# Unused space at both edges of SBUF moves where a three-stage kernel's tiles begin

## The chip, the cores and the metric

One core of one Trainium2 chip. The metric is the device time of one execution in microseconds, as a median of the runs.

## What is computed

Three stages follow one another on 2,304 tokens, all in fp32 (batch 4, 8 heads, 576 positions, head width 64; model width 512; hidden width 2,048):

```python
# attention by a feature map
proj = x @ w_phi;  proj -= max(abs(proj))
phi(x) = concat(exp(proj), exp(-proj))
kv = phi(k).T @ v;  z = sum(phi(k))
attn = (phi(q) @ kv) / (phi(q) @ z + 1e-6)
# first layer
h = x @ w_in1;  x = (h * cos(h)) @ w_out1
# second layer
h = x @ w_in2;  out = (max(h, 0) + alpha * min(h, 0)) @ w_out2
```

q, k, v, the four weights (float64) and alpha come from HBM; the host only lays out q, k and v.

## The kernel before, in words

Every fp32 product of the two layers is made of three matmuls (`mm3`, L163): each operand is split into a high and a low part (xh and xl, wih and wil, woh and wol, gh and gl), and high·high, high·low and low·high are added in PSUM. The parts have type fp32r.

The tokens stand in five groups, four of 512 and one of 256 (`groups`). The hidden width stands in 16 tiles of 128 (ft). One step is one ft for one group in one layer, 160 steps in all (`steps`). A step computes

- `hidden`: a tile ph of 128 hidden units × the group's tokens, 4 kk × 3 = 12 matmuls; the moving rows are xh or xl of one kk (512 or 256 columns), the stationary operand is a 128 × 128 slice of wih or wil;
- `turns`, `gate` and `activate` (ScalarE, VectorE), which end with gh (a ScalarE copy, L85) and gl (a GpSimd subtraction, L86);
- `output`: the products with the second weight into the PSUM tiles po. In layer 0 the moving rows are gh or gl, the stationary slices are from woh or wol, 4 × 3 = 12 matmuls; in layer 1 the moving rows are woh or wol (always 512 columns), the stationary slices are from gh or gl, 12 matmuls for a group of 512 tokens and 6 for the one of 256.

The order is written by hand (`tc.manual_schedule()`, `moe_step`): hidden runs five steps ahead of output, and on TensorE a sequence of ph matmuls follows a sequence of po matmuls. Weights are decoded from float64 by ten instructions on three engines (`w_instructions`), at times that a small planner in the kernel sets, into six slots per kind. The weight loads go through SyncE's queue (`fetch_w`).

Where a tile lies is set by the order of the pools. Pools are stacked from both ends of SBUF. From the left: `const` (small constants, w2 and ident of the attention), `small`, `xpool` (xh and xl, four rows of 2,304 fp32 each), `wst` and `wtmp` (staging of the weights), `wpool` (weight slots 0 and 1), `accp` (five accumulators), then the attention's `wk` and `qpp`, which make room later for `wpool2` (slots 2 to 5) and `wtmp2`. From the right: the attention's `vp` and `kw`, which make room later for `gp` (five gh and five gl) and `mt` (two r). A weight tile, gh, gl and r have 2,048 bytes in each partition; xh and xl have 36,864, which is 18 × 2,048.

Of the kernel before, what the change touches and what calls it, by code (L numbers as in the profile page):

```python
# [10 lines left out]
F32 = mybir.dt.float32  # L11
# [10 lines left out]
P = 128  # L22
# [6 lines left out]
def feature_map_attention_two_mlps(  # L29
# [30 lines left out]

    ctx.enter_context(tc.manual_schedule())

    const = ctx.enter_context(tc.tile_pool(name="const", bufs=1))
    small = ctx.enter_context(tc.tile_pool(name="small", bufs=2))
    xpool = ctx.enter_context(tc.tile_pool(name="xpool", bufs=1))
    wst = ctx.enter_context(tc.tile_pool(name="wst", bufs=2))
# [731 lines left out]
```

## Time and profile before

| | us |
|---|---|
| time, median of 3 runs | 998.44 (998.33 to 998.99) |
| span of the profiled execution, first to last instruction | 996.2 |
| TensorE busy | 989.7 |
| its weight loads busy | 838.6 |
| VectorE, GpSimd, ScalarE busy | 686.3, 606.4, 493.9 |

The profiled execution has its span alone, not a device time of its own; the median stands 2.2 us above the span. In the views, PE is TensorE's matmuls and PEld its weight loads, DVE is VectorE, ACT ScalarE, POOL GpSimd. L163 is line 163 of the kernel. A name like po<-gh,wol reads: the output tile, the moving tile, the stationary tile. A matmul's duration is the time from its issue to its modelled end; the next begins before that.

### The profile page before, as it was taken

How to read it: one execution, taken by the hardware profiler on the slowest of the kernel's cores; microseconds unless marked ns; L12 is line 12 of the kernel's file. 1: busy time of each engine (PE TensorE's matmuls, PEld its weight loads, DVE VectorE, ACT ScalarE, POOL GpSimd, SP SyncE). 2: the span in 40 equal slices, each digit the busy share in tenths (PEclk: the TensorE clock that was granted, in tenths of full speed). 3: DMA queues.
4: the chain of work that ended last, by engine and by line, in shares of the span. 5: the costliest groups of instructions: out<-in, count | busy, mean ns of one | idle time of the engine just before them, and what ended most of it. 6: DMA issues, size and time to landing. Idle time of an engine off the chain costs nothing.

```text
span 996.2 us, 13997 instructions
## 1 busy us (share of the span) xinstructions
PE 989.7 (99%) x5145; PEld 838.6 (84%) x5145; DVE 686.3 (69%) x976; ACT 493.9 (50%) x967; POOL 606.4 (61%) x498
## 2 busy tenths in 40 slices
PE   9999999999999999999999999999999999999998
PEld 7999999888888888888888888888888888888886
DVE  6868686668886577647764789587748774875343
ACT  5888888866666476646665663132213221322100
POOL 3577787856667366536655889477537753775221
PEclk9999999999999999999999999999999999999999
DMA  6454543211111021101110111011101110110112
GB/s 166 108 149 120 151 126 91 71 44 60 64 43 64 22 63 44 43 22 62 44 43 22 43 59 48 22 62 45 43 22 58 50 43 22 50 55 1 43 58 91
DMA packets 64580, 60.63 MB, mean 61 GB/s; under 512 B 28928, under 2 KB 54656, under 8 KB 64512
## 3 DMA queue, kind: packets, MB, share of 16 engines
q1 hardware_dynamic: 64512, 59.75, 20.0%
q8 instruction: 40, 0.66, 0.3%
q14 instruction: 28, 0.23, 0.1%
HBM read 52.50 MB, written 4.79 MB: 58 GB/s over the span
## 4 chain that ended last, share of the span: by engine, by line
PE 96%; DVE 1%; ACT 1%; issue 1%; POOL 1%; POOLq 0%; ACTq 0%
PE ph L163 39%; PE po L163 39%; PE pj L453 6%; PE kv L494 5%; PE nm L578 5%; PE tp L534 2%; PE tp L430 0%; DVE acc L243 0%; ACT acc L553 0%; DVE wt L125 0%; DVE wt L122 0%; DVE we L126 0%; ACT qp1h L567 0%; POOL wol L133 0%; POOL gl L86 0%
## 5 line engine op out<-in xcount | busy, mean ns | idle before, releaser
L86 POOL TENSOR_TENSOR gl<-r,gh 128x512 fp32r<-128x512 f32 (+1 forms) x160 | 204.1, 1277 | 305.4 <-ACT gh L85 300.4
L85 ACT CAST gh<-r 128x512 fp32r<-128x512 f32 (+1 forms) x160 | 92.1, 576 | 392.9 <-DVE r L209 266.9
L163 PE MATMUL ph<-xh,wil 128*128 128x512 f32 (+1 forms) x640 | 236.7, 370 | 0.0
L163 PE MATMUL ph<-xh,wih 128*128 128x512 f32 (+1 forms) x640 | 236.5, 370 | 0.0
L163 PE MATMUL ph<-xl,wih 128*128 128x512 f32 (+1 forms) x640 | 236.0, 369 | 0.0
L243 DVE TENSOR_TENSOR acc<-po,acc 128x512 f32<-128x512 f32 (+1 forms) x134 | 86.9, 658 | 104.7 <-PE po L163 104.1
L163 PEld LDWEIGHTS ph<-xl,wih 128*128 128x128 f32 x640 | 120.5, 188 | 22.3 <-POOL xl L622 0.2
L163 PEld LDWEIGHTS ph<-xh,wih 128*128 128x128 f32 x640 | 120.5, 188 | 22.0
L163 PEld LDWEIGHTS ph<-xh,wil 128*128 128x128 f32 x640 | 120.4, 188 | 21.3
L163 PE MATMUL po<-gh,wol 128*128 128x512 f32 (+1 forms) x320 | 119.5, 373 | 0.1
L163 PE MATMUL po<-gh,woh 128*128 128x512 f32 (+1 forms) x320 | 119.0, 372 | 0.0
L163 PE MATMUL po<-gl,woh 128*128 128x512 f32 (+1 forms) x320 | 119.0, 372 | 0.0
L163 PE MATMUL po<-woh,gh 128*128 128x512 f32 x288 | 114.0, 396 | 0.0
L163 PE MATMUL po<-woh,gl 128*128 128x512 f32 x288 | 113.6, 394 | 0.1
L163 PE MATMUL po<-wol,gh 128*128 128x512 f32 x288 | 113.6, 395 | 0.0
L122 DVE SCALAR_TENSOR_TENSOR wt<-ws,we 128x512 int32<-128x512 int32 x64 | 97.9, 1530 | 2.4
L196 DVE TENSOR_SCALAR r<-ph,al 128x512 f32<-128x512 f32 (+1 forms) x80 | 55.3, 691 | 58.0 <-PE ph L163 38.1
L131 POOL TENSOR_TENSOR wu<-wu,we 128x512 f32<-128x512 f32 x64 | 83.0, 1297 | 1.3 <-ACT wu L128 1.3
L207 DVE TENSOR_TENSOR r<-ph,r 128x512 f32<-128x512 f32 (+1 forms) x80 | 50.5, 631 | 47.8 <-ACT r L194 47.7
L569 POOL TENSOR_TENSOR qp1l<-acc,qp1h 128x512 fp32r<-128x512 f32 (+1 forms) x64 | 59.1, 949 | 26.4 <-ACT qp1h L567 26.4
L494 PEld LDWEIGHTS kv<-vm,kp 128*128 128x128 f32 x512 | 72.3, 191 | 2.6 <-ACT qp1h L567 0.4
L494 PE MATMUL kv<-vm,kp 128*128 128x66 f32 x512 | 72.2, 255 | 0.1
(81 smaller groups left out, 1876.0 us busy)
## 6 DMA issues: line engine op xcount, KB each, us to landing
ws<-in_moe_w_in_dram SPq DMA_DIRECT2D x32, 512.0 KB, 3.6
ws<-in_moe_w_out_dram SPq DMA_DIRECT2D x32, 512.0 KB, 3.5
acc<-dr SPq DMA_DIRECT2D x32, 144.0 KB, 3.0
out_dram<-acc SPq DMA_DIRECT2D x18, 256.0 KB, 2.0
vm<-in_v_dram SPq DMA_DIRECT2D x16, 256.0 KB, 3.5
kin<-in_k_dram SPq DMA_DIRECT2D x28, 128.0 KB, 2.8
qin<-in_q_dram SPq DMA_DIRECT2D x28, 128.0 KB, 2.8
acc<-acc SPq DMA_DIRECT2D x16, 144.0 KB, 2.4
```

The source lines that it names most:

```text
L85: nc.scalar.copy(hi, src)
L86: lo_engine.tensor_tensor(out=lo, in0=src, in1=hi.bitcast(F32), op=ALU.subtract)
L122: lambda: stt(out=t, in0=w1, scalar=-0x40000000, in1=e, op0=ALU.bitwise_and, op1=ALU.bitwise_or),
L131: lambda: tt(out=u, in0=u, in1=ef, op=ALU.mult),
L163: nc.tensor.matmul(ps, lhsT=l, rhs=r, start=(first and m == 0), stop=(last and m == n - 1))
L196: nc.vector.tensor_scalar(out=r, in0=ph, scalar1=0.0, scalar2=al[:, ft:ft + 1], op0=ALU.min, op1=ALU.mult)
L207: nc.vector.tensor_tensor(out=r, in0=ph, in1=r, op=ALU.mult)
L243: nc.vector.tensor_tensor(out=a, in0=po, in1=a, op=ALU.add)
L453: nc.tensor.matmul(pj[:, a].rearrange("p j f -> p (j f)"), lhsT=x[:, a * P:(a + 1) * P], rhs=w2.rearrange("p j f -> p (j f)"), start=True, ...
L494: nc.tensor.matmul(ps[:, :, y, :] if pr is None else ps[:, pr, y, :], lhsT=e[:, s, 2 * a + y, :], rhs=vt[:, y] if pr is None else vm[:, pr ...
L569: nc.gpsimd.tensor_tensor(out=dl, in0=et, in1=dh.bitcast(F32), op=ALU.subtract)
L578: nc.tensor.matmul(nm, lhsT=l[:, s, pr, y * VW:(y + 1) * VW], rhs=r[:, s, y, :], start=(s == 0 and m == 0), stop=(s == 1 and m == 2),)
```

## The change

Two tiles are allocated that no instruction reads or writes: one of 504 fp32 per partition in a new pool at the right edge, ahead of all others there, and one of 40 fp32 at the head of the left-most pool.

```diff
     ctx.enter_context(tc.manual_schedule())
 
+    edge = ctx.enter_context(tc.tile_pool(name="edge", bufs=1, side="right"))
+    edge.tile([P, 504], F32, name="edge")
     const = ctx.enter_context(tc.tile_pool(name="const", bufs=1))
+    const.tile([P, 40], F32, name="fill")
     small = ctx.enter_context(tc.tile_pool(name="small", bufs=2))
     xpool = ctx.enter_context(tc.tile_pool(name="xpool", bufs=1))
```

Afterwards x, the layers' weights and the gated tiles all begin at multiples of 2,048 bytes.

## Rows read from the trace of the kernel before

**Rows 1.** The page: the span, and busy time by engine.

```profile
span 996.2 us, 13997 instructions
PE 989.7 (99%) x5145; PEld 838.6 (84%) x5145; DVE 686.3 (69%) x976; ACT 493.9 (50%) x967; POOL 606.4 (61%) x498
```

**Rows 2.** The page: the chain that ended last, by engine and by line.

```profile
PE 96%; DVE 1%; ACT 1%; issue 1%; POOL 1%; POOLq 0%; ACTq 0%
PE ph L163 39%; PE po L163 39%; PE pj L453 6%; PE kv L494 5%; PE nm L578 5%; PE tp L534 2%; PE tp L430 0%; DVE acc L243 0%; ACT acc L553 0%; DVE wt L125 0%; DVE wt L122 0%; DVE we L126 0%; ACT qp1h L567 0%; POOL wol L133 0%; POOL gl L86 0%
```

**Rows 3.** TensorE's longest wait (us, times, longest); the page's costliest GpSimd group.

```profile
PE tp L430 <- DVE half_pi L432: 1.5, 1, 1.5
...
L86 POOL TENSOR_TENSOR gl<-r,gh 128x512 fp32r<-128x512 f32 (+1 forms) x160 | 204.1, 1277 | 305.4 <-ACT gh L85 300.4
```

**Rows 4.** Stages: us, busy us by engine, granted clock, DMA share, GB/s.

```profile
0.00:196.00 196.00, 193.75 (x1421) 178.74 (x1422) 142.49 (x241) 158.96 (x366) 138.13 (x136) 1.00 0.48 123
...
242.00:600.00 358.00, 357.95 (x1721) 298.92 (x1720) 252.95 (x350) 215.56 (x387) 227.13 (x179) 1.00 0.14 46
...
700.00:980.00 280.00, 280.00 (x1281) 231.03 (x1281) 175.02 (x231) 59.54 (x108) 143.74 (x111) 1.00 0.12 42
```

**Rows 5.** Matmuls of L163 by shape: count | busy us, mean ns | idle before.

```profile
L163 PE MATMUL ph<-xh,wih 128*128 128x512 f32 x512 | 200.5, 392 | 0.0
...
L163 PE MATMUL po<-woh,gh 128*128 128x512 f32 x288 | 114.0, 396 | 0.0
...
L163 PE MATMUL po<-gh,wol 128*128 128x512 f32 x256 | 101.3, 396 | 0.1
...
L163 PE MATMUL ph<-xl,wih 128*128 128x256 f32 x128 | 36.2, 283 | 0.0
...
L163 PE MATMUL po<-gh,wol 128*128 128x256 f32 x64 | 18.2, 284 | 0.0
```

**Rows 6.** The chain in order of time, layer 0: start us, us, what.

```profile
441.81 2.79 PE po L163 x12
444.60 2.73 PE ph L163 x12
447.33 1.44 PE po L163 x12
448.77 2.76 PE ph L163 x12
```

**Rows 7.** The same in layer 1.

```profile
702.74 2.80 PE po L163 x12
705.54 2.76 PE ph L163 x12
...
722.20 1.43 PE ph L163 x12
```

**Rows 8.** Matmuls in order of time, layer 1: start us, duration us.

```profile
702.58 0.40 PE L163 MATMUL po<-woh,gh 128*128 128x512 f32 x1
702.82 0.40 PE L163 MATMUL po<-wol,gh 128*128 128x512 f32 x1
703.05 0.39 PE L163 MATMUL po<-woh,gl 128*128 128x512 f32 x1
...
707.22 0.39 PE L163 MATMUL ph<-xh,wil 128*128 128x512 f32 x1
707.44 0.39 PE L163 MATMUL ph<-xh,wih 128*128 128x512 f32 x1
707.67 0.39 PE L163 MATMUL ph<-xl,wih 128*128 128x512 f32 x1
```

**Rows 9.** The chain in order of time, in the attention: start us, us, what.

```profile
15.39 1.30 PE pj L453 x6
```

**Rows 10.** Weight loads by shape: count | busy us, mean ns | idle before.

```profile
L163 PEld LDWEIGHTS ph<-xh,wih 128*128 128x128 f32 x640 | 120.5, 188 | 22.0
```

## The prediction

> **What bounds the kernel now.** I first read the page's busy times [rows 1]: TensorE is busy for 99% of the span, its weight loads for 84%, GpSimd for 61%. That share is modelled, so I check it against the chain that ended last [rows 2]: 96% of it is TensorE, 39% hidden products (ph), 39% output products (po), and nothing else above 6%. The third view is what TensorE waited for: 1.5 us in the longest entry, while GpSimd alone waited 300.4 us for the gated tile that it subtracts [rows 3]. The other engines have slack; TensorE has none. The fourth is the table of stages [rows 4]: the granted clock is 1.00 in every stage, the 2.4 GHz level, so no time is to be had from the clock. The attention ends at about 196 us; the two layers fill the remaining 800 us of a span of 996.2.
>
> So the time is a count of matmuls times the distance between their starts. The by-shape table gives the counts [rows 5]: 3 × 512 for ph with 512 columns, 3 × 288 and 3 × 256 for po, together 3,168; with 256 columns 3 × 128 and 3 × 64, together 576. The distance must not be read off the duration column: 392 ns is the latency of one matmul, and matmuls overlap. The chain in order of time shows it. In layer 0 twelve po take 2.79 us and twelve ph 2.73, where they follow 512-column po [rows 6], or 232.5 and 227.5 ns each; in layer 1 it is 2.80 and 2.76 [rows 7]. 512 columns at 2.4 GHz are 213.3 ns. Each matmul thus pays 14 to 20 ns over its columns, and po pays more than ph. Single starts say how [rows 8]: 240, then 230 ns at the head of a po sequence, 220 and 230 at the end of the next ph sequence (starts rounded to 10 ns). The distances wander inside a sequence although nothing is waited for.
>
> **What the change does, part by part.** No instruction, DMA, wait or buffer is added or removed; two tiles that nobody reads or writes take space. `fill` (40 × 4 = 160 bytes) lifts everything on the left that is allocated after it; `edge` (504 × 4 = 2016 bytes) lowers everything on the right. If x, the weights and the gated tiles begin at multiples of 2048 afterwards, then before x and the weights began 2048 − 160 = 1888 bytes past one, gh and gl 2016 bytes past one (all are made of whole 2048-byte pieces). From the shapes: a row of x for one kk is 2304 × 4 = 9216 bytes, so odd kk begin 1024 further; a weight slice begins at a multiple of 512 from its tile.
>
> TensorE reads two streams, the moving rows and the next weights, and only their addresses change. In ph both are on the left: their starts differ by a multiple of 512 bytes, before and after. In po one is on the left and one on the right: they differ by a multiple of 512 plus or minus 128 before (2016 − 1888), by a plain multiple of 512 after. This is the one relation that changes, and it splits the matmuls as the trace does: ph is the quicker one in both layers, although in layer 1 po has the weights as its moving rows and in layer 0 the gated tiles [rows 6, 7].
>
> Costs, step by step. The two tiles themselves: nothing, no instruction touches them. VectorE, ScalarE and GpSimd read other addresses too; whatever this is worth, up or down, lies under TensorE while the 300.4 us of slack stand [rows 3]; without that cover the 1277 ns of the GpSimd subtraction [rows 3] would come due per step, but a step of 24 matmuls lasts over 5.5 us. DMAs land at other offsets, all issued a tile ahead: nothing. Attention: no relation that I can price; I leave it at 196 us and let the range carry it.
>
> The matmuls: bounds from rows. No gain at all is one end. The other is the pace of the attention's projections, whose passes take 1.30 / 6 = 216.7 ns [rows 9], 3.4 over 213.3; they are of another number format, so this is a far row. With 216.7 for 512 columns and 110 for 256, twelve become 2.60 and 1.32. Layer 0: 64 sequences (4 groups × 16) of each kind, 64 × (0.13 + 0.19) = 20.5 us; layer 1: 64 × 0.16 + 72 × 0.20 = 24.6 (its 864 po are 72 dozens); 256 columns: 48 dozens from about 1.43 [rows 6, 7] to 1.32, 5.3. Sum 50.4. Losses are not excluded: the nearest row is the 240 ns at the head of a po sequence [rows 8].
>
> By the Trainium skill ("TensorE: Matmul & The Clock Gate", Back-to-back issue gap) a warm matmul follows the last after N / 2.4 + 2.5 ns, 215.8 for 512 columns; no 512-column matmul of these layers runs so here, and by that page the most to be had would be an estimated 53 us.
>
> I take the value nearest to the changed relation: all twelves go to the quickest that this kernel has at 512 columns, 2.73 us [rows 6]. Layer 0 po: 64 × 0.06 = 3.8; layer 1 ph: 64 × 0.03 = 1.9 (slow only in its first half, which follows a po); layer 1 po: 72 × 0.07 = 5.0. Sum **10.8 us**. The median of the runs is 998.44, the profiled span 996.2, so 2.2 us lie around the span and stay. 998.4 − 10.8 = 987.6, say **988**. What is late next is again TensorE: 10.8 us over 128 steps is 0.08 us a step.
>
> **Rivals.**
> *No effect.* The 14 to 20 ns belong to the matmul itself (its number format, its weight swap) and the wandering to the PE's own pipeline. For it: with 256 columns a ph's moving rows cross a multiple of 2048 in the even kk alone and a po's always, yet a dozen takes 1.43 and 1.44 us [rows 6, 7]. Against it: po and ph differ at 512 columns with equal shapes. Time 998.4. The Trainium skill speaks for it ("TensorE: Matmul & The Clock Gate", Step-by-step: what each phase is for): moving rows and weights have read ports of their own, and loading the next weights takes nothing from the running matmul. By that rule my 10.8 us would be zero; the trace neither agrees nor disagrees, since every matmul here has a weight load beside it [rows 10].
>
> *Full pace.* The start offset costs each matmul a fixed piece, whatever its length: 1.43 / 12 − 106.7 = 12.5 ns at 256 columns and 227.5 − 213.3 = 14.2 at 512 are nearly the same [rows 6, 7]. Before the change all these operands begin 32 bytes off a multiple of 64 (1888 and 2016 are); aligned, the piece goes in part or whole: 998.4 − 50.4 = 948 at most, half of it 973. Against it: a fixed piece is also what a swap would cost.
>
> *Lockstep (slower).* Moving rows and next weights now always begin at the same place of their 2048 bytes, or whole slices apart, and collide at their starts in every po. Price: the 240 ns of the worst po [rows 8] for all, 2.88 a dozen: 64 × 0.09 + 72 × 0.08 = 11.5 us, 1010. It decides from 0.65 ns a matmul on (2 us / 3,168). For it: the page's chain gives no reason for 240. Against it: ph has had this relation all along and is the quicker.
>
> *Inert.* An untouched tile might get no space; then 998.4.
>
> **How the numbers follow.** Settled pace (988, with half or all of the gain and a little more: 984 to 996) 0.36; no effect 0.27; full pace 0.17; lockstep 0.18; inert 0.02. About 0.2%, 2 us, is what a measurement of this kernel can tell from no change. Faster 0.36 + 0.17 = 0.53; same 0.27 + 0.02 = 0.29; slower 0.18. The range takes the first two cases whole, the full pace down to 958 (0.12 of it) and lockstep up to half its price, 1004 (0.07): 0.82 or so. The likeliest case's own range is 984 to 996.
>
> **What would show it.** Right: dozens of po at 2.73 to 2.76 in both layers, ph 2.73 in layer 1 as in layer 0, 256-column dozens still 1.43, the attention still 196 us, the granted clock 1.00. No effect: 2.79 and 2.80 stand. Full pace: 256-column dozens under 1.38 and ph under 2.70. Lockstep: po dozens above 2.82 while ph stays. I am wrong altogether if the time changes while the dozens don't: then it lies in the attention, or in a wait that TensorE has not had.

## The result, and the profile after

The changed kernel takes 988.35 us as a median of 4 runs (987.32 to 989.85), the kernel before 998.38 beside it: a ratio of 0.9896, 95% interval 0.9884 to 0.9907, that is 10.0 us less. 988 was forecast.

The page of the profiled execution, in the parts that answer to [rows 1] and [rows 2]: span and busy time, then the chain by engine.

```profile
span 987.3 us, 13997 instructions
PE 979.3 (99%) x5145; PEld 838.7 (85%) x5145; DVE 689.2 (70%) x976; ACT 494.2 (50%) x967; POOL 607.4 (62%) x498
...
PE 95%; ACT 2%; DVE 1%; issue 1%; POOL 1%; DMA 0%; POOLq 0%; ACTq 0%
```

Every count is the old one, the weight loads cost the same, and TensorE is the bound as before; its busy time alone went from 989.7 to 979.3. The duration column by shape says little of this (it answers to [rows 5]; count, busy us, mean ns): 392 ns has become 390 and 396 has become 390. It shows latency, which no sum of the time can use.

```profile
L166 PE MATMUL ph<-xh,wih 128*128 128x512 f32 x512 | 199.5, 390 | 0.0
...
L166 PE MATMUL po<-woh,gh 128*128 128x512 f32 x288 | 112.4, 390 | 0.0
...
L166 PE MATMUL po<-gh,woh 128*128 128x512 f32 x256 | 99.8, 390 | 0.0
```

The chain in order of time (start us, us, what) is where it shows. First layer 0, as [rows 6], then layer 1, as [rows 7]:

```profile
441.40 2.72 PE po L166 x12
444.12 2.72 PE ph L166 x12
446.84 1.43 PE po L166 x12
448.28 2.75 PE ph L166 x12
...
709.56 2.72 PE po L166 x12
712.28 2.72 PE ph L166 x12
715.00 2.72 PE po L166 x12
717.72 1.43 PE ph L166 x12
719.16 2.75 PE po L166 x12
```

po has fallen from 2.79 and 2.80 to 2.72, ph of layer 1 from 2.76 to 2.72, and the two kinds now run alike. 256-column dozens stay at 1.43. The single starts of a po sequence of layer 1 (start us, duration us), beside [rows 8]: where distances of 240 and 230 ns stood at its head, every one is now 220 or 230 by the rounded starts.

```profile
709.40 0.39 PE L166 MATMUL po<-woh,gh 128*128 128x512 f32 x1
709.63 0.39 PE L166 MATMUL po<-wol,gh 128*128 128x512 f32 x1
709.85 0.39 PE L166 MATMUL po<-woh,gl 128*128 128x512 f32 x1
710.08 0.39 PE L166 MATMUL po<-woh,gh 128*128 128x512 f32 x1
```

One thing is new and costs time. TensorE's waits, and the place in its order of time:

```profile
PE ph L166 <- POOL xl L625: 1.1, 1, 1.1
...
212.51 0.38 PE L166 MATMUL ph<-xh,wih 128*128 128x256 f32 x1 [0.35 <-ACT xh L623]
214.00 0.38 PE L166 MATMUL ph<-xl,wih 128*128 128x256 f32 x1 [1.10 <-POOL xl L625]
```

The last row of x comes out of the attention, is split by ScalarE and GpSimd, and is then needed by the first products of the group of 256 tokens in layer 0. TensorE now stands still for it twice, 1.45 us together; by the distance of starts against the kernel before it costs 1.7. The attention itself ends 0.6 us later than before (the first ph dozen starts at 188.82 in place of 188.19); why is open. The start of the same matmul thus lies 2.27 us later than before at 212.8 us of the old span, and 8.69 us earlier at 981 us of it: between the two the layers gain 11.0 us. 11.0 − 2.3 = 8.7 of the 8.9 us between the spans.

### The profile page after: what moved, and what is told of

Its sections match the earlier page's. It is cut to its first block, busy times and chain, and to the rows that moved or that the text cites. A ratio compares the mean times of both kernels' runs of the same rounds, so it can differ in the third digit from the quotient of the medians.

```text
span 987.3 us, 13997 instructions
## 1 busy us (share of the span) xinstructions
PE 979.3 (99%) x5145; PEld 838.7 (85%) x5145; DVE 689.2 (70%) x976; ACT 494.2 (50%) x967; POOL 607.4 (62%) x498
## 4 chain that ended last, share of the span: by engine, by line
PE 95%; ACT 2%; DVE 1%; issue 1%; POOL 1%; DMA 0%; POOLq 0%; ACTq 0%
PE po L166 39%; PE ph L166 38%; PE pj L456 6%; PE kv L497 5%; PE nm L581 5%; PE tp L537 2%; PE tp L433 0%; DMA dn<-acc 0%; ACT acc L556 0%; DVE r L193 0%; DVE wt L128 0%; ACT acc L594 0%; ACT r L196 0%; ACT r L185 0%; ACT r L197 0%
```

## The experiments

**Theory A**, after the prediction: while a matmul streams its moving rows, the next weights are loaded beside it, and the two disturb one another unless their starts differ by a multiple of some number of bytes; I took 512. Its rivals: B, each stream must begin at a multiple of 64 bytes; C, 512 columns must not cross a multiple of 2048 bytes. All experiments edit the two allocations of the changed kernel or the text shown, and all were timed in three rounds beside the kernel before on the same chip. "Left" is x and the weights, "right" is gh, gl and r.

**Four pairs of offsets.** Nothing at the left edge and 128 bytes at the right:

```diff
-    edge.tile([P, 504], F32, name="edge")
+    edge.tile([P, 32], F32, name="edge")
-    const.tile([P, 40], F32, name="fill")
```

> Left tiles stay 1888 bytes past a multiple of 2048, the right ones go from 2016 to 1888: the two sides agree, but nothing begins at a multiple of 64. Theory A (what counts is that moving rows and weights begin a multiple of 512 bytes apart): the whole gain, 988, dozens of 2.72 to 2.73 us for po and ph in both layers. Theory B (what counts is that each stream begins at a multiple of 64 bytes): no gain, 998, po at 2.79 and 2.80. Theory C (what counts is that 512 columns don't cross a multiple of 2048 bytes): no gain, 998.

Measured 987.83 us, ratio 0.9891 (0.9876 to 0.9905).

Only the left edge:

```diff
-    edge = ctx.enter_context(tc.tile_pool(name="edge", bufs=1, side="right"))
-    edge.tile([P, 504], F32, name="edge")
```

> The left tiles begin at multiples of 2048, the right ones stay 2016 past one. Theory A: the sides differ by 32 bytes, no gain, 998, po still at 2.79 and 2.80. Theory B: layer 0 po (moving rows right, weights left) and layer 1 po (the other way round) each have one bad stream; at most part of the gain, 993 to 998, ph in layer 1 at 2.72 at its end. Theory C: layer 1 po (moving rows left, at multiples of 2048) falls to 2.72, layer 0 po stays at 2.79: 998.4 - 5.8 = about 993.

Measured 998.11, ratio 0.9997 (0.9988 to 1.0006).

Only the right edge:

```diff
-    const.tile([P, 40], F32, name="fill")
```

> The right tiles begin at multiples of 2048, the left ones stay 1888 past one. Theory A: the sides differ by 160 bytes, no gain, 998. Theory B: one bad stream in each po, ph as before: 994 to 998. Theory C: layer 0 po (moving rows right) falls to 2.72, layer 1 po stays at 2.80: 998.4 - 4.5 = about 994.

Measured 1000.19, ratio 1.0019 (1.0009 to 1.0028): a little slower than before.

Both sides aligned, but 128 bytes apart:

```diff
-    edge.tile([P, 504], F32, name="edge")
+    edge.tile([P, 472], F32, name="edge")
```

> The left tiles begin at multiples of 2048, the right ones 128 bytes past one, so that both begin at multiples of 64 and 128 but differ by 128, as before the change. Theory A: no gain, 998, po at 2.79 and 2.80 as before. Theory B: the whole gain, 988. Theory C: layer 1 po alone falls to 2.72, about 993.

Measured 998.17, ratio 0.9996 (0.9987 to 1.0006).

B and C fall by the first and the fourth: with nothing aligned and every long read crossing 2048 bytes the whole gain is there, and with the left at multiples of 2048 and the right at a multiple of 128 none is. The chain of the first, in layer 1, and under it that of the fourth, in both layers:

```profile
702.83 2.72 PE po L165 x12
705.55 2.72 PE ph L165 x12
```

```profile
464.23 2.79 PE po L166 x12
467.02 2.73 PE ph L166 x12
...
702.84 2.80 PE po L166 x12
705.63 2.76 PE ph L166 x12
```

The fourth has the dozens of the kernel before [rows 6, 7] to the hundredth, though all its addresses are others: only the difference is the same. The third differs by 160 bytes and is worse by up to two hundredths a dozen:

```profile
442.36 2.81 PE po L165 x12
...
692.58 2.80 PE po L165 x12
695.38 2.77 PE ph L165 x12
```

**Is it the two sides, or the two streams?** 128 unused bytes between x and everything behind it, and the right side moved along:

```diff
-    edge.tile([P, 504], F32, name="edge")
+    edge.tile([P, 472], F32, name="edge")
     xpool = ctx.enter_context(tc.tile_pool(name="xpool", bufs=1))
+    gap = ctx.enter_context(tc.tile_pool(name="gap", bufs=1))
+    gap.tile([P, 32], F32, name="gap")
     wst = ctx.enter_context(tc.tile_pool(name="wst", bufs=2))
```

> x stays at multiples of 2048; 128 unused bytes behind it put all else on the left, the weights too, and the gated tiles on the right 128 bytes past one. So weights and gated tiles agree (po), while x and the weights, both on the left, differ by 128 (ph). Theory A (a matmul's moving rows and the weights loaded beside it must begin a multiple of 512 bytes apart): po keeps 2.72, ph goes to 2.79 or 2.80 in both layers, 988.3 + 128 x 0.075 = about 998. Rival (only the two sides of SBUF must agree, whatever lies within a side): 988, all dozens at 2.72. Rival (ph is quick for a reason of its own, such as its 12 matmuls into one PSUM bank): ph stays at 2.72 and the time at 988.

Measured 998.10, ratio 0.9998 (0.9988 to 1.0008). Its chain in layer 0 and in layer 1:

```profile
465.24 2.74 PE po L168 x12
467.98 2.79 PE ph L168 x12
...
703.72 2.73 PE po L168 x12
706.45 2.79 PE ph L168 x12
```

ph and po have changed places. Both of ph's tiles lie on the left, so the side plays no part, and ph is not quick for a reason of its own.

**The period.** The right side at 256, 512 and 64 bytes past a multiple of 2048:

```diff
-    edge.tile([P, 504], F32, name="edge")
+    edge.tile([P, 440], F32, name="edge")
```

> As the changed kernel, but the right side begins 256 bytes past a multiple of 2048: the sides differ by 256. Theory A with a period of 512 bytes: no gain, 998, po at 2.79 to 2.81. With a period of 256 or less: the whole gain, 988.

Measured 987.94, ratio 0.9898 (0.9883 to 0.9912).

```diff
-    edge.tile([P, 504], F32, name="edge")
+    edge.tile([P, 376], F32, name="edge")
```

> As the changed kernel, but the right side begins 512 bytes past a multiple of 2048. Theory A with a period of 512 bytes (ph has such differences already, between one kk and the next): the whole gain, 988, dozens of 2.72. If tiles must begin at the same place of 2048 bytes: no gain, 998.

Measured 987.53, ratio 0.9893 (0.9879 to 0.9908).

```diff
-    edge.tile([P, 504], F32, name="edge")
+    edge.tile([P, 488], F32, name="edge")
```

> As the changed kernel, but the right side begins 64 bytes past a multiple of 2048. Differences of 32, 128 and 160 bytes gave nothing, 0, 256 and 512 all. Theory A with a period of 256 bytes: no gain, 996 to 1000, po at 2.77 to 2.82. Rival (what hurts is a difference of half a period, 128, and an odd number of 32s): 64 is harmless, 988.

Measured 998.20, ratio 0.9999 (0.9990 to 1.0009). Differences of 0, 256 and 512 bytes give the whole gain, 32, 64, 128 and 160 none. 512, as I had it, was too strict: the period is 256 bytes. The moving rows of po lie on the right in layer 0 and on the left in layer 1, so each difference was tried with both signs; 32, 64, 128 and 160 either way are, within 256 bytes, every multiple of 32 but 0, and at each of them a dozen of po takes 2.76 us or more. At 64 the loss is shared out differently, 2.76 for po (a little under the 2.77 to 2.82 expected) and 2.77 for ph in layer 0, 2.80 and 2.75 in layer 1:

```profile
464.76 2.76 PE po L166 x12
467.52 2.77 PE ph L166 x12
...
703.37 2.80 PE po L166 x12
706.17 2.75 PE ph L166 x12
```

**Do the other engines have a part in it?** r, which TensorE never reads, moved alone:

```diff
+                gap = ctx.enter_context(tc.tile_pool(name="gap", bufs=1, side="right"))
+                gap.tile([P, 32], F32, name="gap")
                 pools["mt"] = ctx.enter_context(
```

> As the changed kernel, but r, which ScalarE, VectorE and GpSimd use and TensorE never reads, lies 128 bytes off; x, weights, gh and gl as in the changed kernel. Theory A (TensorE's own two streams): 988, dozens of 2.72. Rival (the other engines' accesses to the right side disturb TensorE): some of the gain is lost, 990 to 998.

Measured 987.46, ratio 0.9893 (0.9879 to 0.9908): the whole gain. Moving r by 128 bytes is of no account.

**One matmul or the sequence?** gl moved alone, by a spacer between gh and gl in their pool:

```diff
-    edge.tile([P, 504], F32, name="edge")
+    edge.tile([P, 472], F32, name="edge")
...
         gh = pools["gp"].tile([P, 512], F32R, tag="gh", name="gh")[:, 0:n]
+        if j == 0:
+            pools["gp"].tile([P, 32], F32, tag="sp", name="sp", bufs=1)
```

> As the changed kernel, but gl alone lies 128 bytes off; gh, x and the weights as in the changed kernel. Theory A (each matmul's moving rows against the weights loaded beside it, period 256 bytes): only the matmuls with gl are off, a third of po: po dozens near 2.72 + 0.075 / 3 = 2.745, ph 2.72, time 988 + 136 x 0.025 = about 991.5. If it is the next matmul's weights that count, the long distances of layer 1 stand at woh x gh just ahead of a gl load and not at the matmul with gl itself. Rival (one tile out of place upsets the whole sequence): po dozens back at 2.79, about 998 less what ph gained.

Measured 991.43, ratio 0.9933 (0.9919 to 0.9948). The sum said 991.5, and that it came so near is luck: by the distance of starts, against the changed kernel, the stretch from 212.8 to 604 us of the old span (layer 0) lost 0.9 us, where the sum has 64 × 0.025 = 1.6, and that from 604 to 981 (layer 1) lost 3.3, where it has 72 × 0.025 = 1.8. The chain, layer 0 and layer 1, and single starts of layer 1:

```profile
462.98 2.75 PE po L166 x12
465.73 2.72 PE ph L166 x12
...
704.86 2.77 PE po L166 x12
707.63 2.72 PE ph L166 x12
```

```profile
704.70 0.39 PE L166 MATMUL po<-woh,gh 128*128 128x512 f32 x1
704.92 0.40 PE L166 MATMUL po<-wol,gh 128*128 128x512 f32 x1
705.16 0.40 PE L166 MATMUL po<-woh,gl 128*128 128x512 f32 x1
705.39 0.39 PE L166 MATMUL po<-woh,gh 128*128 128x512 f32 x1
```

The loss does not take in the whole sequence. In layer 0, with gl as moving rows, one of three is long: the distance that follows the eighth matmul of a dozen (gl) is 234.1 ns in the mean of the 46 dozens that follow a 512-column ph, those after the ninth and tenth are 225.9 and 226.6 (from the starts in the trace). In layer 1, where gl is loaded as weights, two of three are long: 232.4 after wol × gh, beside which gl is loaded, and 234.2 after woh × gl itself (eighth and ninth place, means of 47 such dozens), against 226.7 after woh × gh (tenth place). My expectation named the wrong matmul as the one ahead of a gl load (it is wol × gh). It also asked whether the matmul's own weights or the next ones count. The first long distance speaks for the load that runs beside the matmul; why the second one stays long, when gh is loaded beside it, is open.

Nor is the loss confined to the matmul that is out of step: it runs on into matmuls whose own streams are in step. In layer 1 of the kernel before, the distances of a ph dozen behind po are 235.8, 224.2, 230.8, 235.9, 228.4, 232.4 and 230.7 ns, and only from the eighth matmul on 226.6 to 226.9 (means of the 43 dozens of 2.76). The twelfth is long again, 232.4; beside it the first gh of the next po is loaded, while in layer 0, where woh is loaded there, it is 226.7. The 2.77 of ph in layer 0 at 64 bytes reads as such an after-effect through ten of twelve places (its own streams are in step), and so do the 2.74 and 2.73 of po in the run with x moved off. A dozen behind a 256-column sequence also starts slow (233.2, 235.8, 228.5, 232.5, 231.0, then 226.5 for ph of layer 0 in the changed kernel), though all is in step there.

**The rest over 213.3 ns, and the number format.** All matmuls of the two layers read 2-byte elements, with the tiles of the changed kernel and with those of the kernel before:

```diff
+                l, r = (z.bitcast(BF16)[:, 1::2] for z in (l, r))
                 nc.tensor.matmul(ps, lhsT=l, rhs=r, start=(first and m == 0), stop=(last and m == n - 1))
```

> As the changed kernel, but every matmul of the two layers reads the upper halves of its operands as bf16 (every second 2-byte element of the same bytes); the products are those of the cut operands. This asks what the 13 ns are that each 512-column matmul still pays over its 213.3 ns. If they belong to the fp32r operands: dozens near 12 x 216.7 = 2.60, 988 - 264 x 0.12 - 48 x 0.11 = about 951. If they belong to the change of weights in the array: dozens stay at 2.72, 988.

> The kernel before with the same bf16 reading of every matmul operand of the two layers. If the relation between the two streams matters for whatever TensorE reads: slower than its twin with aligned tiles by about 10 us. If it matters only for fp32r: both take the same time within 2 us.

Measured 978.12 (ratio 0.9795, 0.9781 to 0.9810) and 978.41 (0.9801, 0.9786 to 0.9815), so the same within 0.3 us. The chain in layer 0, first with the aligned tiles, then with those of before:

```profile
461.48 2.70 PE ph L167 x12
464.18 2.70 PE po L167 x12
```

```profile
463.48 2.71 PE po L164 x12
466.18 2.70 PE ph L164 x12
```

With 2-byte elements the relation between the streams counts for hardly anything: a dozen of po takes 2.71 where fp32r takes 2.79 at the same addresses. That answers the second expectation: the disturbance comes with the fp32r operands and not with the addresses alone. Whether it is their width, their format or the step of two that makes the difference, no run separates. The first came out between its two answers, nearer to 988: 225 ns a matmul against 226.7, still 11.7 over the columns. Elements at a step of two may have a price of their own, so what the remaining piece is stays open; that it goes away with an aligned start is excluded by every run with aligned tiles.

## Why the prediction was right

**What bounds the kernel.** The chain and the counts held: the gain came from the distance of starts on TensorE, and only the 2.3 us lost ahead of 212.8 us came from elsewhere. The granted clock was 1.00 throughout.

**The changed relation.** The argument was that only po's two streams change against one another, and that po would then run like ph. The first four runs show this as the cause and not a coincidence: equal offsets without alignment have the gain, alignment with unequal offsets has not. The run with x moved off shows the other half, that ph owed its pace to the same relation. What in the chip makes the two streams disturb one another at such distances, no run shows.

**The sum.** 10.8 us were forecast, 10.0 measured, 11.0 gained in the layers. The mechanism was right; that the number is so near is in part luck. Dozens in step fell to 2.72 and not 2.73: the 2.73 of ph in layer 0, taken as the settled pace, still held three long distances behind po (231.7, 232.5 and 230.8 ns). With 2.72 the three terms would give 64 × 0.07 + 64 × 0.04 + 72 × 0.08 = 12.8, and ph of layer 0, which the sum has at nothing, 64 × 0.01 = 0.6 more. But dozens behind a 256-column sequence stood at 2.76 to 2.79 and fell to 2.75 only, and a quarter of layer 1's ph dozens stood at 2.73 already, so the counts of 64 and 72 were too many. By the distance of starts layer 0 gained 4.8 us, where the sum has 3.8, and layer 1 6.2, where it has 6.9.

**What is late next.** "Again TensorE" missed one place: at 212 us the last row of x ends last in the profiled execution. TensorE reaches its ph there with next to no slack (the kernel before waits 0.2 us on its weight load at the same spot), and whether it waits depends on when the attention's end comes out: the run with the right side at 512 doesn't have this wait. The run with gl moved has it too, 1.1 us; the first of the four pairs has 0.3 of it, the runs at 256 bytes and with r moved none. The two executions with 1.1 took 989.06 and 992.38 us, 1.7 and 1.0 above the lowest of their kernels. That the changed kernel's runs spread over 2.5 us and those of before over 0.7 would fit with it, but only one execution of each kernel has a trace.

**The rivals.** No effect, lockstep and inert are out by the result. Lockstep had the sign wrong: equal starts are the good case, as ph already showed. (The 0.65 ns from which it was to decide should be 1.2: 2 us over the 1,632 po of 512 columns, the only ones that it touches.) Full pace named alignment as the cause and fell with the first run; the fixed piece that it counted on is still there, 13.3 ns over the columns at both lengths once a sequence has settled (120.0 and 226.7 ns). Its bound of 50.4 us also rested on a wrong row: the projections that take 216.7 ns have 256 columns in the trace, so they give no pace for 512. The Trainium skill ("TensorE: Matmul & The Clock Gate", Step-by-step: what each phase is for), by which loading the next weights takes nothing from the running matmul, is not borne out for these fp32r reads: 2.79 against 2.72 a dozen with no other difference than where the two begin. With 2-byte elements the trace agrees with it, 2.71 against 2.70.

## What to carry to other kernels

When TensorE is busy without a gap, measure the distance of matmul starts, not their durations, and compare the kinds of matmul with one another: here the kind that was slower at equal shapes had the cause in where its operands begin. In this kernel sequences of fp32r matmuls with 512 columns lose about 6 ns a matmul, 2.5%, unless moving rows and weights begin a multiple of 256 bytes apart, and some of it falls on the matmuls behind them; with 256 columns no loss shows (dozens of po of 1.41 to 1.44 us out of step, 1.43 in step). 128 unused bytes at one edge of SBUF were enough to put it right (987.83 us), and alignment to 2048 was not needed. A small tile put ahead of others moves every later tile: making the unused tile at the right edge 64 bytes smaller cost the whole 1% again (998.20 us).

## What the runs showed of the hardware that I had not expected

- The period is 256 bytes: 0, 256 and 512 apart give 987.5 to 988.4 us, 32, 64, 128 and 160 apart give 998.1 to 1000.2.
- The disturbance repeats exactly: the run with both sides aligned but 128 bytes apart has the kernel before's dozens of 2.79, 2.73, 2.80 and 2.76 at wholly different addresses.
- The disturbance outlasts its cause. With fp32r weights out of step, the matmul after the one beside which they are loaded is long as well, 234.2 against 226.7 ns; behind po out of step, ph in step takes up to ten matmuls to come back to 226.7.
- With 512 columns, fp32r matmuls in step and bf16 matmuls at a step of two both stand 12 to 13 ns over 213.3 (226.7 and 225); with 256 columns it is 13 for fp32r (120.0 over 106.7) but 7 for bf16 (113.3).
